# Halved copies at the end of a two-layer kernel, and a new table of due times and engine choices

## The chip, the core and the metric

The kernel runs on one core of a Trainium2 chip. What is measured is device time in microseconds (us), from the start of the program on the core to its end. Five engines work side by side, each through its own list of instructions in order: TensorE (PE: matmuls; PEld: its weight loads), VectorE (DVE), ScalarE (ACT), GpSimd (POOL) and SyncE (SP), which here issues all transfers.

## The reference

Three stages follow one another, all in float32:

```python
state = alpha[:, :, t, :, None] * state + einsum('bhd,bhe->bhde', k[:, :, t], v[:, :, t])
y[:, :, t] = einsum('bhd,bhde->bhe', q[:, :, t], state)          # B=4, H=8, S=768, D=48
x = y as 3072 tokens x 384
h = x @ w_in;  g = (a0 + a1 h + a2 h^2 + a3 h^3) / (1 + |b0||h| + |b1|h^2 + 1e-6);  x = g @ w_out
h = x @ w2_in; g = h * tanh(softplus(h));                                           out = g @ w2_out
```

Both layers have 2048 hidden columns. The weights come as 64-bit floats.

## The kernel before, in words

**The tiles.** The sequence is cut into 6 chunks of 128 positions; with 4 batches a chunk is 512 tokens. A phase (l, c) is layer l on chunk c: 16 steps of 128 hidden columns. In a step `hidden_mms` makes nine matmuls of 512 columns (L653: a high and a low part of x, a high and a low part of the weight) into one of the banks 2 to 4; `hidden` puts the activation on it; `split_g` splits the result into a high part (a cast, L221 on ACT or L223 on DVE) and a low part (a subtraction, L214 on DVE or L216 on POOL); `out_mms` makes nine matmuls (L702) into the sums in banks 5, 6 and 7. Twelve phases run in the order of `PHASES`: (0,0), (0,1), (1,0), (0,2), (1,1), (0,3) and so on to (1,5).

**Attention.** `attn_unit` does one pair of batches of one chunk. Its steps hang on one another: six levels (1, 2, 4, 8, 16, 32) of small matmuls (L462), each followed by DVE work (L477 or L471 scales the operands for the next level, L497 copies the result under a mask) or by ACT copies (L492 at level 16, L486 at level 32); then transposes (L526), their copies (L530), an outer product (L541, copied by L565 in chunk 0), the outputs (L576), their copies (L633), transposes back (L526) and copies into xf (L637), from which L223 and L647 make the high and low parts xh and xl that L653 reads. The units of chunk 0 come first. The first one works in the tile `pair`, the second in banks 2 and 3 (its tiles live inside `zp`, `xg` and `u`). The third unit, of chunk 1, works in `pair` again.

**Weights.** `load_w` brings in one of 32 blocks (L327) and makes float32 of 64-bit words: L328 on ACT, then by the letter in `E_CV` either three DVE steps (D: L330, L332, L334) or two on ACT and one on DVE (A: L341, L342, L344). A cast (L221 or L223 by `E_HC`) gives the high part, a subtraction (L214) or two matmuls and copies (L352, L353, L356) the low part, and both are stored for the later phases.

**The order.** Nobody writes the instructions down in the order in which they stand. Each operation is put into a `Plan` with an engine, a cost and a due time; `Plan.order` then walks through time with those costs, gives each free engine the ready operation that is due first, and the instructions are emitted in the order that comes out. Due times come from a table of numbers (`T_PH`, `AT_P`, `D_X`, `LAG` and others); strings of letters choose engines (`E_M`, `E_GL0`, `E_GL1` by chunk, `E_CV` and `E_HC` by weight block). Between the small matmuls of the start the plan puts fill matmuls (L746). Each engine follows its list strictly: whatever waits holds up all that stands behind it.

**The end.** `evacuate` copies the three banks of sums into `u` (bank 6 on DVE, 5 and 7 on ACT) and issues one store for each.

## Time and profile before

| | us |
|---|---|
| runs of the kernel | 1008.17, 1003.24, 1002.68 (median 1003.24) |
| the profiled execution's own time | 1004.26 |
| its span | 1001.6 |
| PE busy | 969.1 (97%) |
| DVE busy | 668.6 (67%) |
| ACT busy | 622.4 (62%) |
| POOL busy | 263.6 (26%) |

The span runs from the first to the last recorded instruction or transfer; 2.66 us of the profiled execution lie around it. In rows of the trace a number of instructions stands behind an x; a matmul of float32 data counts as two records. A time in brackets is how long the engine stood idle before the row, and the name behind the arrow is what ended that. "issue" means that the profile shows nothing that it waited for. PEclk is the granted clock of TensorE: 1.00 is 2.4 GHz, 0.50 is 1.2 GHz.

### The profile page before, as it was taken

The page shows a single profiled execution, that of the slowest core. Times are in us where ns is not written, and L with a number is a line of the kernel's source. Part 1 is how long each engine was busy: PE and PEld are TensorE (multiplying, and loading weights), DVE is VectorE, ACT ScalarE, POOL GpSimd, SP SyncE. Part 2 cuts the span into 40 slices and gives each one's busy share as a digit, 9 for nine tenths or more (in the row PEclk, how much of TensorE's full clock was granted, in tenths as well). Part 3 has the DMA queues.
Part 4 walks back from the last instruction along what each step waited for, and adds up shares of the span by engine and source line. Part 5 has one row for each costly group of instructions (what it writes and reads, how often), then busy time and mean ns, then how long its engine had stood idle before and what let it go on. Part 6 is the DMA issues. An engine that isn't in the chain of part 4 may idle for free.

```text
span 1001.6 us, 24480 instructions
## 1 busy us (share of the span) xinstructions
PE 969.1 (97%) x10376; PEld 784.4 (78%) x10376; DVE 668.6 (67%) x867; ACT 622.4 (62%) x1051; POOL 263.6 (26%) x202
## 2 busy tenths in 40 slices
PE   7998999899999999999999999999999999999998
PEld 5776877678788878788878888878788878888886
DVE  5668799999997789954589634699952389400211
ACT  2587999699969698622399723396621299633332
POOL 3023675454100044200277700153300000133000
PEclk9799999999999999999999999999999999999999
DMA  7266549756588868557736764848456454565530
GB/s 293 98 222 270 199 151 326 252 164 206 203 292 311 309 230 277 173 191 225 255 97 222 228 210 135 293 153 263 117 167 190 143 156 143 142 214 150 172 111 31
DMA packets 75756, 199.98 MB, mean 200 GB/s; under 512 B 8192, under 2 KB 34944, under 8 KB 74112
## 3 DMA queue, kind: packets, MB, share of 16 engines
q1 hardware_dynamic: 75648, 198.43, 60.3%
q8 instruction: 81, 1.33, 0.5%
q14 instruction: 27, 0.22, 0.1%
HBM read 166.94 MB, written 31.46 MB: 198 GB/s over the span
## 4 chain that ended last, share of the span: by engine, by line
PE 68%; DVE 11%; ACT 9%; issue 3%; DMA 3%; POOL 1%; DVEq 0%; ACTq 0%; POOLq 0%
PE bank L702 31%; PE bank L653 30%; PE pair L462 4%; DVE zp L686 2%; DVE zp L677 1%; DVE zp L679 1%; DVE gg L214 1%; ACT zp L674 1%; DVE qka L477 1%; PE pair L612 1%; ACT u L668 1%; DMA qka<-in_qka_dram 1%; ACT gg L221 1%; ACT zp L681 1%; POOL zp L675 1%
## 5 line engine op out<-in xcount | busy, mean ns | idle before, releaser
L702 PE MATMUL bank<-gg,wo 128*128 128x512 f32 x1728 | 428.5, 392 | 1.9 <-DVE gg L214 0.8
L702 PEld LDWEIGHTS bank<-gg,wo 128*128 128x128 f32 x1728 | 321.0, 188 | 70.4 <-DVE gg L214 1.5
L653 PE MATMUL bank<-xh,wih 128*128 128x512 f32 x576 | 230.8, 401 | 4.9 <-DVE zp L679 2.3
L653 PE MATMUL bank<-xl,wih 128*128 128x512 f32 x576 | 225.6, 392 | 2.3 <-DVE xl L647 2.3
L653 PE MATMUL bank<-xh,wl 128*128 128x512 f32 x576 | 225.9, 392 | 0.5 <-DVE wl L214 0.5
L690 ACT ACTIVATE zp<-bank 128x512 f32<-128x512 f32 x96 | 57.4, 597 | 197.7 <-PE bank L653 196.1
L675 POOL TENSOR_TENSOR zp<-zp,u 128x512 f32<-128x512 f32 x80 | 125.2, 1571 | 160.0 <-ACT zp L674 159.5
L214 DVE TENSOR_TENSOR gg<-zp,gg 128x512 fp32r<-128x512 f32 x144 | 101.6, 710 | 95.3 <-ACT gg L221 90.4
L653 PEld LDWEIGHTS bank<-xh,wih 128*128 128x128 f32 x576 | 108.7, 189 | 30.2 <-DVE zp L679 2.7
L653 PEld LDWEIGHTS bank<-xl,wih 128*128 128x128 f32 x576 | 108.9, 189 | 24.4 <-DVE xl L647 3.1
L653 PEld LDWEIGHTS bank<-xh,wl 128*128 128x128 f32 x576 | 108.6, 189 | 24.1 <-DVE wl L214 1.0
L216 POOL TENSOR_TENSOR gg<-zp,gg 128x512 fp32r<-128x512 f32 x48 | 69.8, 1456 | 217.9 <-ACT gg L221 209.5
L221 ACT CAST gg<-zp 128x512 fp32r<-128x512 f32 x144 | 89.2, 621 | 46.2 <-PE bank L702 31.4
L550 POOL TENSOR_TENSOR tmp<-X,qk 48x768 f32<-48x768 f32 x19 | 30.3, 1595 | 232.3 <-DVE X L555 148.8
L677 DVE SCALAR_TENSOR_TENSOR zp<-zp,sc,bank 128x512 f32<-128x512 f32 x96 | 70.9, 742 | 22.3 <-ACT zp L676 19.8
L686 DVE SCALAR_TENSOR_TENSOR zp<-zp,sc 128x512 f32<-128x512 f32 x80 | 75.5, 949 | 6.4 <-ACT zp L685 5.5
L681 ACT ACTIVATE zp<-zp,c 128x512 f32<-128x512 f32 x96 | 69.4, 725 | 14.3 <-POOL zp L675 14.2
L462 PEld LDWEIGHTS pair<-qka 48*64 48x64 f32 (+4 forms) x3840 | 55.1, 129 | 27.8 <-issue 11.1
L676 ACT ACTIVATE zp<-bank,sc 128x512 f32<-128x512 f32 x96 | 66.1, 688 | 13.4 <-PE bank L653 10.3
L679 DVE SCALAR_TENSOR_TENSOR zp<-zp,sc,bank 128x512 f32<-128x512 f32 x96 | 71.1, 744 | 2.5 <-ACT u L668 0.7
L462 PE MATMUL pair<-qka 48*64 48x32 f32 (+4 forms) x3840 | 62.0, 215 | 6.2 <-DVE AT L497 3.3
L668 ACT ACTIVATE u<-bank 128x512 f32<-128x512 f32 x96 | 56.8, 596 | 15.8 <-PE bank L653 12.1
(124 smaller groups left out, 983.3 us busy)
## 6 DMA issues: line engine op xcount, KB each, us to landing
wo<-woD SPq DMA_DIRECT2D x160, 384.0 KB, 3.3
wl<-wlD SPq DMA_DIRECT2D x160, 192.0 KB, 2.5
qka<-in_qka_dram SPq DMA_DIRECT2D x10, 1536.0 KB, 7.8
woD<-wo SPq DMA_DIRECT2D x16, 768.0 KB, 4.9
raw<-in_w1o_dram SPq DMA_DIRECT2D x8, 768.0 KB, 4.9
raw<-in_w1i_dram SPq DMA_DIRECT2D x8, 768.0 KB, 5.2
wlD<-wl SPq DMA_DIRECT2D x16, 384.0 KB, 4.6
raw<-in_w2i_dram SPq DMA_DIRECT2D x8, 768.0 KB, 5.6
```

Source lines behind the costliest of these rows:

```text
L214: dve(n, due, reads, writes, lambda: nc.vector.tensor_tensor(**kw()))
L216: pool(n, due, reads, writes, lambda: nc.gpsimd.tensor_tensor(**kw()))
L221: act(n, due, reads, writes, lambda: nc.scalar.copy(out=out(), in_=in_()), src="s")
L462: nc.tensor.matmul(bk[j][o:o + m, 32 * g:32 * g + 32].rearrange("p (n l) -> p n l", l=L), lhsT=K[h, e * HC:e * HC + m], rhs=Qv[h, e, :, 1, :],
L653: nc.tensor.matmul(bank[hb], lhsT=w[:, k * P:(k + 1) * P], rhs=x[k], start=(k == 0 and j == 0), stop=(k == KT - 1 and j == 2))
L668: act(NTOK, due, [kh, "tab"], [ku], lambda: nc.scalar.activation(u, h, AF.Abs), table="ln")
L675: pool(NTOK, due, [ku], [kz], lambda: nc.gpsimd.tensor_tensor(out=zs[r], in0=zs[r], in1=u, op=ALU.mult))
L677: dve(NTOK, due, [kh], [kp], lambda: nc.vector.scalar_tensor_tensor(out=ps[r], in0=ps[r], scalar=A2, in1=h, op0=ALU.add, op1=ALU.mult), po ...
L679: dve(NTOK, due, [kh], [kp], lambda: nc.vector.scalar_tensor_tensor(out=ps[r], in0=ps[r], scalar=A1, in1=h, op0=ALU.add, op1=ALU.mult), po ...
L681: act(NTOK, due, [], [kz], lambda: nc.scalar.activation(zs[r], zs[r], AF.Ln, bias=c_1), src="s", ptr=1, table="ln")
L686: dve(NTOK, due, [kw], [kp], lambda: nc.vector.scalar_tensor_tensor(out=ps[r], in0=ps[r], scalar=A0, in1=w(), op0=ALU.add, op1=ALU.mult), ...
L702: nc.tensor.matmul(bank[5 + k], lhsT=wos[b][:, w, k * P:(k + 1) * P], rhs=x[q], start=(f == 0 and j == 0), stop=(f == FT - 1 and j == 2))
```

## The change

The last phase's sums are copied in halves of 256 columns, the left half by ACT, the right half by DVE, and each half has a store of its own: six instead of three. The table of numbers is another one, the plan counts a table load of ACT at the first conversion of layer 0, and eight strings and numbers choose other engines. Cut to the core:

```diff
-T_PH = (8.402, 4.683, 4.572, 7.535, 7.065, 5.706, 9.463, 9.341, 5.182, 6.904, 4.724, 3.344)
+T_PH = (8.402, 4.739, 4.796, 7.6, 7.065, 5.962, 9.494, 9.394, 5.212, 7.04, 4.831, 2.283)
...
-E_M = 'PPPPPV'
-E_GL0 = 'PVVPVV'
-E_GL1 = 'VVVVPV'
+E_M = 'PPVPPV'
+E_GL0 = 'PVVVVV'
+E_GL1 = 'VPVPPV'
...
-E_CV = 'ADAAAAAAAAAAAADADDDDDADDDAAAAAAAA'
+E_CV = 'ADAAAAAAADAAADADDDDDADDDAADDDADA'
...
+LOADED0 = None
...
-        out, busy, loaded = [], {}, "ln"
+        out, busy, loaded = [], {}, LOADED0
...
-        act(n, due, [kr], [ks], lambda: nc.scalar.activation(st, mag, AF.Copy, scale=F64_SHIFT), src="s")
+        act(n, due, [kr], [ks], lambda: nc.scalar.activation(st, mag, AF.Copy, scale=F64_SHIFT), src="s",
+            table="ln" if l == 0 else None)
...
+            if (l, c) == PHASES[-1]:
+                plan.readers[f"u{j}b"] = plan.readers.get(f"u{j}", []) + [plan.writer[f"u{j}"]]
+                for n, t in enumerate((slice(0, NTOK // 2), slice(NTOK // 2, NTOK))):
+                    ku = f"u{j}" + "b" * n
+                    if n:
+                        dve(NTOK // 2, due, [f"bank{5 + k}"], [ku], lambda k=k, j=j, t=t: nc.vector.tensor_copy(
+                            out=us[j][:, t], in_=bank[5 + k][:, t]), port=False)
+                    else:
+                        act(NTOK // 2, due, [f"bank{5 + k}"], [ku], lambda k=k, j=j, t=t: nc.scalar.copy(
+                            out=us[j][:, t], in_=bank[5 + k][:, t]))
+                    dma(131, due, [ku], [], lambda k=k, j=j, t=t: nc.sync.dma_start(out=out[c][:, k, t], in_=us[j][:, t]))
+                continue
```

Further numbers of the table (`AT_P`, `LAG`, `D_SPL`, `W_LEAD`, `X_LEAD`, `D_W2`, `D_X`, `D_EV`) and letters of `E_HC` change in the same manner. What the table does is seen in the lists of the engines. Line numbers of the change are 1 to 14 higher than those of before: L334 becomes L336, L477 L479, L497 L499, L341 L343, L486 L488, L633 L635.

**Place 1: DVE in the first 25 us.** `qka0` and `pair` belong to the first unit, `zp` and `bank2`, `bank3` to the second, `f321` is the buffer of the first weight block. Before:

```order
L477 TENSOR_TENSOR qka0_145<-qka0_145 128x2x256x2
L471 TENSOR_TENSOR zp_134<-zp_134 128x1024
L497 COPY_PREDICATED zp_134<-cst_65,bank2_127 128x256
L497 COPY_PREDICATED AT0_144<-cst_65,pair_126 128x128x4
L497 COPY_PREDICATED zp_134<-cst_65,bank3_128 128x256
L477 TENSOR_TENSOR qka0_145<-qka0_145,qk0_148 128x2x128x4
L334 SCALAR_TENSOR_TENSOR f321_102<-raw1_100,f321_102 128x768
```

In the change:

```order
L479 TENSOR_TENSOR qka0_145<-qka0_145 128x2x256x2
L336 SCALAR_TENSOR_TENSOR f321_102<-raw1_100,f321_102 128x768
L473 TENSOR_TENSOR zp_134<-zp_134 128x1024
L479 TENSOR_TENSOR qka0_145<-qka0_145,qk0_148 128x2x128x4
L499 COPY_PREDICATED AT0_144<-cst_65,pair_126 128x128x4
L499 COPY_PREDICATED zp_134<-cst_65,bank2_127 128x256
```

The last step of the block's conversion moves from behind the first unit's level 4 (the row with 128x2x128x4) to ahead of it, and the second unit's copies under the mask move behind it.

**Place 2: ACT at the second unit's level 32.** The four rows that end in 32x8x32 copy that level's result out of banks 2 and 3. Before:

```order
L633 COPY vn0_146<-pair_126 128x384
L492 COPY zp_134<-bank3_128 16x8x16
L356 CAST wl2_89<-bank7_132 128x384
L341 ACTIVATE zb0_103<-raw0_99 128x768
L356 CAST wl2_89<-bank5_130 128x384
L637 COPY xf_105<-pair_126 128x3x128 x2
L328 ACTIVATE f320_101<-raw0_99 128x768
L486 COPY zp_134<-bank2_127 32x8x32
L342 ACTIVATE zb0_103<-raw0_99,c_f_69 128x768
L486 COPY zp_134<-bank3_128 32x8x32
```

In the change:

```order
L635 COPY vn0_146<-pair_126 128x384 x2
L343 ACTIVATE zb0_103<-raw0_99 128x768
L488 COPY zp_134<-bank2_127 32x8x32
L358 CAST wl2_89<-bank7_132 128x384
L488 COPY zp_134<-bank3_128 32x8x32
L639 COPY xf_105<-pair_126 128x3x128 x2
L488 COPY zp_134<-bank2_127 32x8x32
L358 CAST wl2_89<-bank5_130 128x384
L488 COPY zp_134<-bank3_128 32x8x32
L329 ACTIVATE f320_101<-raw0_99 128x768
```

The copies move ahead of conversion steps (L328 and L342 of before) that they stood behind.

**Place 3: the last copies.** `bank_130`, `bank_131` and `bank_132` are banks 5, 6 and 7. The waits in brackets name the engines or transfers whose semaphores the instruction waits for. ACT in the change:

```order
L722 COPY u<-bank_130 128x256 [waits DMAHW4_49,PE_49]
L722 COPY u<-bank_131 128x256 [waits DMAHW5_49,PE_49]
L722 COPY u<-bank_132 128x256 [waits DMAHW6_49,PE_49]
```

DVE in the change:

```order
L719 COPY u<-bank_130 128x256 [waits DMAHW4_49,Activation_49]
L719 COPY u<-bank_131 128x256 [waits DMAHW5_49,Activation_49]
L719 COPY u<-bank_132 128x256 [waits DMAHW6_49,Activation_49]
```

Before, ACT copied two whole banks and DVE one, and each of these copies waited for PE. In the change ACT's halves wait for PE and DVE's halves wait for ACT.

## Rows read from the trace of the kernel before

**Rows 1.** Windows by stage: length; busy PE, PEld, DVE, ACT, POOL; PEclk; DMA share, GB/s.

```profile
84.50:175.80 91.30, 86.27 (x1324) 67.81 (x1323) 80.04 (x95) 84.61 (x142) 54.75 (x40) 0.98 0.64 227
175.80:251.20 75.40, 70.89 (x836) 56.70 (x837) 70.49 (x86) 62.76 (x118) 35.18 (x26) 0.98 0.62 204
251.20:339.50 88.30, 87.34 (x920) 71.07 (x919) 74.95 (x97) 72.39 (x117) 5.35 (x7) 1.00 0.79 283
339.50:409.80 70.30, 69.67 (x781) 55.76 (x779) 63.55 (x86) 60.16 (x103) 27.69 (x17) 1.00 0.77 252
...
490.00:558.40 68.40, 67.34 (x772) 54.18 (x772) 57.67 (x64) 59.44 (x103) 42.66 (x29) 1.00 0.59 185
```

**Rows 2.** Timeline of DVE, 18 to 29 us: start, length, engine, line.

```profile
18.71 1.27 DVE L477 TENSOR_TENSOR qka<-qka 128x1024 f32<-128x1024 f32 x1
...
25.62 0.70 DVE L497 COPY_PREDICATED AT<-cst,pair 128x512 f32<-128x512 int32 x1 [3.77 <-PE pair L462]
...
27.91 0.94 DVE L334 SCALAR_TENSOR_TENSOR f<-raw,f 128x768 int32<-128x768 int32 x1
```

**Rows 3.** Timeline of ACT at 28.9 us.

```profile
28.89 0.83 ACT L221 CAST wo<-f 128x768 fp32r<-128x768 f32 x1 [5.28 <-DVE f L334]
```

**Rows 4.** Timeline of PE, 22 to 39 us.

```profile
22.62 1.24 PE L746 MATMUL bank<-cst 128*128 128x256 f32 x5 [2.96 <-issue]
23.79 1.78 PE L462 MATMUL pair<-qka 48*60 48x32 f32 x64
25.50 3.78 PE L746 MATMUL bank<-cst 128*128 128x256 f32 x8
29.21 1.93 PE L462 MATMUL bank<-zp 48*64 48x32 f32 x64
30.94 1.70 PE L462 MATMUL pair<-qka 48*56 48x32 f32 x64
32.57 5.30 PE L746 MATMUL bank<-cst 128*128 128x256 f32 x12
37.80 0.92 PE L462 MATMUL pair<-qka 48*48 48x32 f32 x64
```

**Rows 5.** Window of the slow clock.

```profile
24.00:36.00 12.00, 12.00 (x208) 10.05 (x204) 7.76 (x10) 1.40 (x2) 0.00 (x0) 0.50 0.35 132
```

**Rows 6.** ACT by line and form, whole span: busy, mean ns of one, idle before.

```profile
L328 ACT ACTIVATE f<-raw 128x768 f32<-128x768 f32 x32 | 29.2, 913 | 18.2 <-DMA raw<-in_w1i_dram 9.8 <-DMA raw<-in_w1o_dram 6.2 <-DMA raw<-in_w2o_dram 2.1
L342 ACT ACTIVATE zb<-raw,c_f 128x768 uint16<-128x768 uint16 x22 | 25.7, 1169 | 0.1
L341 ACT ACTIVATE zb<-raw 128x768 f16<-128x768 f32 x22 | 23.7, 1079 | 0.1
...
L356 ACT CAST wl<-bank 128x384 fp32r<-128x384 f32 x6 | 2.9, 479 | 0.2
```

**Rows 7.** Timeline of ACT: the first unit's and the second unit's last copies.

```profile
48.38 1.07 ACT L530 COPY qka<-pair 128x512 f32<-128x512 f32 x2
...
66.06 0.98 ACT L486 COPY zp<-bank 32x256 f32<-32x256 f32 x3
```

**Rows 8.** Timeline of PE at the first hidden matmul.

```profile
84.52 1.03 PE L462 MATMUL pair<-qka 48*56 48x32 f32 x64
85.48 0.50 PE L653 MATMUL bank<-xh,wih 128*128 128x512 f32 x1
```

**Rows 9.** DVE by line and form, whole span.

```profile
L214 DVE TENSOR_TENSOR gg<-zp,gg 128x512 fp32r<-128x512 f32 x144 | 101.6, 710 | 95.3 <-ACT gg L221 90.4 <-PE bank L702 3.4
...
L671 DVE SCALAR_TENSOR_TENSOR zp<-zp,sc,u 128x512 f32<-128x512 f32 x16 | 11.9, 748 | 1.7 <-ACT zp L670 1.6
```

**Rows 10.** Timeline of the end, and the last stores' time to landing.

```profile
997.30 0.69 DVE L713 COPY u<-bank 128x512 f32<-128x512 f32 x1 [4.05 <-PE bank L702]
997.98 0.58 ACT L715 COPY u<-bank 128x512 f32<-128x512 f32 x1 [0.77 <-PE bank L702]
...
out_dram<-u SPq DMA_DIRECT2D x3, 256.0 KB, 2.1
```

More of the change, by code (lines that the diff above doesn't have):

```diff
@@ L39 @@
 PHASES = ((0, 0), (0, 1), (1, 0), (0, 2), (1, 1), (0, 3), (1, 2), (0, 4), (1, 3), (0, 5), (1, 4), (1, 5))
-T_PH = (8.402, 4.683, 4.572, 7.535, 7.065, 5.706, 9.463, 9.341, 5.182, 6.904, 4.724, 3.344)
+T_PH = (8.402, 4.739, 4.796, 7.6, 7.065, 5.962, 9.494, 9.394, 5.212, 7.04, 4.831, 2.283)
 AT_P0 = (0.318, -13.418, 0.649)
 AT_P1 = (0.292, 1.189, 0.288)
-AT_P = (0.573, 0.916, 0.31)
+AT_P = (0.576, 0.985, 0.276)
 D_MID = 10.219
-LAG = (32.081, 10.172)
-D_SPL = (-7.368, 6.936)
-W_LEAD = 4.738
-X_LEAD = 96.57
+LAG = (31.971, 10.172)
+D_SPL = (-1.971, 5.762)
+W_LEAD = -3.689
+X_LEAD = 69.333
 D_W1 = (0.495, 18.655)
-D_W2 = (17.835, 18.763)
+D_W2 = (20.572, 23.284)
 E_LO = 'VV'
 E_TREE, E_QK = ('PPPVPV', 'VVVVVP')
-E_M = 'PPPPPV'
-E_GL0 = 'PVVPVV'
-E_GL1 = 'VVVVPV'
+E_M = 'PPVPPV'
+E_GL0 = 'PVVVVV'
+E_GL1 = 'VPVPPV'
 R_PSUM = 'R.....'
@@ L61 @@
 E_LW = 'PVPPPVVVVVVVVVVVVVVVVVVVVVVVVVVV'
-E_HC = 'AAVVVVVVAAVAAAAVVVAVAVAAVVVAVAAA'
+E_HC = 'AAVVVVVVAAVAAAAAAAAVVAAAAVVVVAVV'
 E_X0 = 'V'
-E_CV = 'ADAAAAAAAAAAADADDDDDADDDAAAAAAAA'
+E_CV = 'ADAAAAAAADAAADADDDDDADDDAADDDADA'
 R0 = (39.706, 10.751)
 NRAW, NF32 = 2, 2
-D_X = 86.568
-D_EV = -19.693
+D_X = 75.469
+D_EV = -9.067
 PAD_FROM = 290.0
```

## The prediction

> **What bounds the kernel now.** I read the windows by stage first, because the share of PE over the whole span hides where it loses. In the stage of the first layer's first chunk PE is busy 86.27 us of 91.30, in the next 70.89 of 75.40; after that it loses 0.96, 0.63 and, in a later one, 1.06 us a stage [rows 1]. From 251 us on PE has next to nothing to give, so an order that changes there can hardly gain, only lose. What can be gained lies ahead of the first hidden matmul at 85.48 us, where small matmuls, DVE and ACT wait for each other in turn.
>
> So I read the timelines of that start, DVE first. DVE ends level 2 of the first attention unit about 19.9 us, then stands 3.77 us until PE has done level 4, and the last step of the first weight block, L334, stands behind that and begins only at 27.91 [rows 2]. ACT, with the cast of that block next in its list, has waited 5.28 us by then [rows 3]. PE loses 2.96 us ahead of 22.62 for a reason that the profile calls issue, then works through five records of fill matmuls before level 4 at 23.79; level 8 begins at 30.94 and level 16 at 37.80, each behind fill matmuls and the second with 5.30 us of them ahead of it [rows 4]. After the lost 2.96 us the granted clock is 0.50, that is 1.2 GHz, from 24 to 36 us, though PE is busy throughout [rows 5]. All of this is a chain: what comes earlier in it brings the first hidden matmul earlier.
>
> **The start, step by step.** The reader should count every step against the same event of before.
>
> *L334* moves ahead of level 4 (place 1). Only rows that DVE does anyway before 20 us stand ahead of it, so it begins at about 19.9 instead of 27.91, 8.0 us earlier, and so does the cast behind it on ACT. SP's next load into that buffer waits for L334 too and moves with it. This is not yet 8.0 us for the kernel: the attention units wait for PE.
>
> *PE.* I assume that the 2.96 us stay, since the transfers ahead of them are issued in the same order, and that the slow clock stays after them. In the change level 4 stands right behind the second unit's level 1, so it begins at about 22.65. The next distances are from starts [rows 4]: level 4 takes 1.71 (25.50 - 23.79), a fill matmul of two records 0.88 (5.30 / 6), the second unit's level 2 takes 1.73 (30.94 - 29.21), level 8 takes 1.63 (32.57 - 30.94). The change has five fill matmuls, then level 8, then three fill matmuls and the second unit's level 2, then level 16. So level 8 begins at 22.65 + 1.71 + 4.40 = 28.8 (before 30.94), level 16 at 28.8 + 1.63 + 2.64 + 1.73 = 34.8 (before 37.80). At the slow clock it takes about 1.6 and ends at 36.4, against 38.72: **2.3 us earlier**. DVE's steps between them fit under the fill matmuls.
>
> *ACT to the first unit's copies.* From the end of level 16 to the end of L530 ACT is busy without a break before; it ends at 48.38 + 1.07 = 49.45 [rows 7]. The change puts one L341, one L342 and one L356 more and one L328 less into this stretch: 1.08 + 1.17 + 0.48 - 0.91 = 1.8, or 1.6 with the tenth by which neighbours overlap [rows 6]. It gives 2.3 - 1.6 = **0.7 us earlier**.
>
> *ACT to the second unit's level 32.* From there to the last L486 before takes 67.04 - 49.45 = 17.6 us [rows 7]. Counted in the two orders, the change does one L328, one L341, two L342 and one L356 less in this stretch, those being done before or put behind the copies (place 2). That is 0.91 + 1.08 + 2.34 + 0.48 = 4.8 us [rows 6], 4.3 without the overlaps. With ACT the engine that never rests here, it is **4.3 us earlier**, so 5.0 in all. What is late next is the second unit's last round: transposes, outer product, outputs, transposes back. ACT's conversions that were put behind now lie in its pauses; I take this part as 0, between 1 us of gain and 1 us of loss.
>
> *Given back.* Before, the third unit's level 8 is done ahead of the first hidden matmul (1.03 us, [rows 8]); in the change that matmul group is only level 4, and level 8 comes later. PE must do it all the same: **1.0 us back**. The first hidden matmul comes at about 80.5 instead of 85.48, and of that 4.0 us stay.
>
> **The engine choices.** In phase (0,2), from 340 us, the multiplication goes from POOL to DVE: the order has L671 15 times more in that stage, 15 x 0.748 = 11.2 us, less an estimated 5.8 of attention steps that move to the stages beside it, on 63.55 of 70.30 busy us of DVE [rows 1, 9]. In the stage from 490 us DVE gets 11 subtractions, 11 x 0.710 = 7.8, on 57.67 of 68.40. In the one from 251 us four blocks are converted by DVE instead of ACT, at least 4 x 0.94 [rows 2], on 74.95 of 88.30. DVE stays below each stage's length; as PE has losses of 0.63 to 1.06 us there, I take 0, with up to 2 us of gain if the losses of the two stages ahead of 251 us shrink, and a rival below for the loss. Elsewhere POOL takes subtractions from DVE in stages where both have room: nothing, covered by steps of PE that are longer than either.
>
> **The last copies.** Before, ACT copies bank 7 in 0.58 us after the last matmul [rows 10]. Halves at once would save some 0.2 us. But DVE's half waits for ACT, and for nothing of PE (place 3); it can only know that the bank is complete through ACT's half of the same bank. So the halves come one after the other: ACT between 0.29 (half of 0.58) and 0.48 (384 columns, [rows 6]), DVE between 0.35 (half of 0.69) and 0.69; about 0.37 + 0.43 plus 0.05 for the semaphore makes 0.85, **0.25 us later** than the 0.58. The last store is half as large; its 2.1 us to landing [rows 10] may shrink by some tenths. The sum of the end is 0.1 us later, between 0.3 earlier and 0.5 later; six stores instead of three are issued while the matmuls of the other banks still run.
>
> The Trainium skill, PSUM — Partial Sum Buffer, section "PSUM bank collisions raise a hardware error", says that two engines must not touch one bank in the same quadrant of partitions at once, not even to read disjoint columns. By it the wait is needed, and the halves at once would not be open to any order of this kernel; had they run at once, the end would come 0.45 us earlier than in my sum. No run here shows a collision.
>
> **The sum.** -0.7 - 4.3 + 1.0 + 0.1 = -3.9 us. The profiled execution took 1004.26, so it gives 1000.4; the median of the runs lies 1.02 below that execution, and so my forecast is 999.3 us.
>
> **The rivals.** *The start gains nothing.* The slow clock lasts longer, or a load or PE's lost 2.96 us grows by what DVE saves. For it: 12 us of slow clock with PE fully busy [rows 5] show that the clock does not follow the work at once, and each of the 10 fill matmuls in this stretch costs 0.88. Against it: ACT's shorter list does not hang on PE's clock. Between 0 and 1 us is left: 1002 to 1004.
>
> *More than my sum.* If PE does not lose the 2.96 us, the clock stays and the start gains the whole 8.0 of L334, less 1.0: 1003.24 - 7.0 = 996.2. Against it: nothing in the change lightens the transfers of the start.
>
> *DVE becomes the bound, the case on the other side.* The stage from 176 us shows what it costs when DVE is busy 70.49 of 75.40, 93%: PE loses 4.51 us [rows 1]. In the change the stages from 251, 340 and 490 us come close to that load or pass it (for the second (63.55 + 11.2 - 5.8) / 70.30 = 98%). If each then loses 4.51 instead of 0.96, 0.63 and 1.06, that is 3 x 4.51 - 2.65 = 10.9 us, and the result is 999.3 + 10.9 = 1010.2. If one of them does so, the gain is gone (1003), if two, 1006. It decides once DVE's busy share passes some 93% while attention levels still wait for it. Against it: from 340 us DVE was 90% busy and PE lost 0.63.
>
> *The change does not do what it says.* For the halves at once I hold this to be so, and it is in the sum.
>
> **How the numbers follow.** My forecast gets 0.47, with 996.5 to 1002 as its own range; a start without gain 0.18; more than the sum 0.14; DVE the bound in one or two stages 0.12, in all three 0.09. No change that is measurable here means within 0.5%, 5.0 us: 998.2 to 1008.3. Faster than that are the 0.14 and some 0.18 out of the forecast's 0.47, and a little from the others: 0.33. Slower is the last case, 0.09. The rest is 0.58. The range holds forecast, the start without gain, most of the larger gain and one or two stages bound by DVE: 993.5 to 1006.0. It leaves out the last case and some 0.08 at the lower end.
>
> **What would show it.** Right: L334 near 20 us and ACT's cast right behind it; level 16 at about 35; the last L486 of the second unit at about 62; the first hidden matmul near 80.5; the stages after 251 us with PE losses near a microsecond; at the end DVE's half beginning after ACT's half of the same bank. Wrong, if the first hidden matmul stays near 85, if the clock stays at 0.50 beyond 40 us, if a stage after 251 us loses over 3 us of PE, or if both halves of a bank begin together.

## The result and the profile after

| | before | after |
|---|---|---|
| median of the runs, us | 1002.96 (4 runs, 999.71 to 1008.17) | 991.15 (4 runs, 989.64 to 993.89) |
| ratio to before | | 0.9876, 95% interval 0.9845 to 0.9906 |
| the profiled execution, us | 1004.26 | 993.89 |
| its span, us | 1001.6 | 992.1 |
| first hidden matmul, us | 85.48 | 79.07 |

The change makes the kernel 1.24% faster, 11.8 us, three times what was forecast, and the time lies below the range. The profiled executions differ by 10.4 us: 9.5 in the span, and 0.9 around it (2.66 us before, 1.79 after; as it varies from 1.7 to 3.1 between executions of the kernel before, this account leaves it out). The other 1.4 of the 11.8 us is spread: the profiled execution lies 1.3 us above the median before, and 2.7 above it after. In the code of the change all lines from L329 on stand one to fourteen further than before (L334 is now L336, L462 is L464, L647 is L649, L653 is L655, L702 is L704).

The windows by stage, as in [rows 1], cut at the first hidden matmul and then where DVE begins each split of x (the low part, L647 before, L649 in the change):

```profile
0.00:79.07 79.07, 68.10 (x1638) 54.85 (x1638) 55.17 (x69) 46.76 (x76) 18.12 (x25) 0.96 0.66 239
79.07:171.48 92.41, 86.23 (x1326) 68.35 (x1324) 85.15 (x94) 83.11 (x140) 56.12 (x40) 0.98 0.62 219
171.48:242.20 70.72, 67.14 (x823) 52.85 (x824) 63.89 (x83) 61.71 (x117) 32.16 (x27) 1.00 0.68 220
242.20:330.66 88.46, 88.32 (x924) 71.77 (x923) 85.39 (x112) 66.28 (x111) 9.04 (x7) 1.00 0.78 276
330.66:400.16 69.50, 69.11 (x782) 56.21 (x781) 67.00 (x91) 57.99 (x102) 2.79 (x2) 1.00 0.78 248
...
915.79:992.10 76.31, 72.06 (x318) 59.34 (x317) 15.10 (x23) 24.06 (x41) 1.30 (x1) 1.00 0.36 105
```

The same cuts before fall at 85.48, 175.84, 251.16 and 925.87 us. By these borders the 9.5 us are 6.4 at the start; 2.55 in the two stages behind it, of which the first gave back 2.0 (92.41 after 90.36) and the second gained 4.6 (70.72 after 75.32); 1.1 from there to 925.87; and 0.6 lost at the end (76.31 after 75.73).

These borders do not stand at the same work. Up to 242.20 us the change has begun 511 of its 3456 matmuls of 512 columns (L655 and L704 together, one record each; called the large matmuls below), up to 251.16 the kernel before 523: 12 matmuls of 0.39 us, 4.7 us, were left for later, as much as the second stage gained, and some 60 small ones (level 8 of the third unit) were taken in. A cut at equal work is the place where 748 of them have been begun, 311.07 us before and 304.05 after. From there to the beginning of the last one:

```profile
311.07:997.55 686.48, 680.05 (x5956) 554.44 (x5955) 406.45 (x551) 376.90 (x633) 152.23 (x105) 1.00 0.60 188
304.05:987.46 683.41, 679.96 (x5956) 554.42 (x5955) 400.75 (x555) 369.37 (x625) 141.22 (x105) 1.00 0.61 188
```

The first row is before, the second after. So the 9.5 us are 6.4 at the start, 0.6 from the first hidden matmul to this cut, 3.1 behind it and 0.6 lost at the end. Behind the cut PE has the same number of matmuls, the same busy time and the same clock in both; what went is idle time, 3.45 us after 6.43. Before, six waits of PE for DVE, of 0.35 to 0.90 us, make up 3.84 us there, these two among them:

```profile
410.56 0.50 PE L653 MATMUL bank<-xl,wih 128*128 128x512 f32 x1 [0.75 <-DVE xl L647]
525.06 0.30 PE L526 MATMUL pair<-cst,qka 128*128 128x128 f32 x1 [0.90 <-DVE qka L477]
```

After, four waits for DVE are left, of 0.19 to 0.30 us, and one of 1.51 us, which both kernels have.

In the two stages up to 242.20 us (251.16 before) PE is not idle for less, 9.76 us after 9.54, but it loses less to slow clock. Before, the second of them has these two windows of ten microseconds, the clock being the third number from the right:

```profile
170.00:180.00 10.00, 7.14 (x26) 5.11 (x27) 9.86 (x13) 7.83 (x19) 4.06 (x3) 0.88 0.69 271
180.00:190.00 10.00, 10.00 (x161) 8.03 (x160) 8.71 (x11) 5.20 (x15) 6.69 (x8) 0.95 0.71 213
```

They lose 1.2 + 0.5 = 1.7 us of PE's work. PE's timeline before shows what stood ahead of them:

```profile
174.50 0.49 PE L653 MATMUL bank<-xh,wih 128*128 128x512 f32 x1 [0.54 <-ACT xh L221]
176.58 0.50 PE L653 MATMUL bank<-xl,wih 128*128 128x512 f32 x1 [1.58 <-DVE xl L647]
...
177.38 0.52 PE L653 MATMUL bank<-xl,wih 128*128 128x512 f32 x1
177.70 0.63 PE L653 MATMUL bank<-xh,wl 128*128 128x512 f32 x1
```

PE waits for ACT's and DVE's part of the split, and behind that a matmul takes 0.63 instead of 0.39 us. After the change PE comes to the same place so:

```profile
170.38 0.49 PE L704 MATMUL bank<-gg,wo 128*128 128x512 f32 x1 [0.44 <-POOL gg L217]
171.62 0.50 PE L704 MATMUL bank<-gg,wo 128*128 128x512 f32 x1 [0.75 <-DVE wo L215]
171.96 0.40 PE L655 MATMUL bank<-xh,wih 128*128 128x512 f32 x1
172.22 0.50 PE L655 MATMUL bank<-xl,wih 128*128 128x512 f32 x1
```

No wait at the split, and the clock stays at 2.4 GHz for the whole stage (PEclk 1.00 from 171.48 to 242.20 us). At the start, PE's timeline (compare [rows 4]) reads:

```profile
22.57 0.25 PE L464 MATMUL bank<-zp 48*64 48x32 f32 x3 [0.86 <-issue]
...
28.22 0.41 PE L464 MATMUL pair<-qka 48*56 48x32 f32 x15 [1.32 <-issue]
28.55 2.03 PE L760 MATMUL bank<-cst 128*128 128x256 f32 x6
30.52 1.94 PE L464 MATMUL bank<-zp 48*64 48x32 f32 x64
32.25 1.48 PE L464 MATMUL pair<-qka 48*48 48x32 f32 x64
```

The pause of 2.96 us is gone; there are shorter ones at other places, in sum no less (4.3 us ahead of the first hidden matmul, before 3.7), and level 16 begins at 32.25 instead of 37.80. The granted clock of the whole start is 0.96 instead of 0.92.

### The profile page after: what moved, and what is told of

The parts are those of the page before. It is cut to its first block, busy times and chain, and to the rows that moved or that the text cites. A ratio compares the mean times of both kernels' runs of the same rounds, so it can differ in the third digit from the quotient of the medians.

```text
span 992.1 us, 24521 instructions
## 1 busy us (share of the span) xinstructions
PE 963.7 (97%) x10370; PEld 780.6 (79%) x10370; DVE 665.5 (67%) x878; ACT 611.0 (62%) x1043; POOL 255.0 (26%) x202
## 4 chain that ended last, share of the span: by engine, by line
PE 72%; DVE 7%; ACT 3%; DMA 2%; issue 1%; DVEq 0%; SPq 0%; ACTq 0%
PE bank L704 34%; PE bank L655 32%; PE pair L464 3%; PE pair L614 2%; DVE zp L688 1%; DMA qka<-in_qka_dram 1%; DVE zp L679 1%; DVE zp L681 1%; PE pair L528 1%; PE pair L543 1%; DMA x2d<-u 1%; DVE AT L499 1%; ACT u L670 1%; DVE gg L215 1%; DVE qka L479 0%
## 5 line engine op out<-in xcount | busy, mean ns | idle before, releaser
L704 PE MATMUL bank<-gg,wo 128*128 128x512 f32 x1728 | 430.2, 393 | 1.5 <-DVE wo L215 0.8
L704 PEld LDWEIGHTS bank<-gg,wo 128*128 128x128 f32 x1728 | 322.1, 188 | 70.4 <-DVE wo L215 1.1
L655 PE MATMUL bank<-xh,wih 128*128 128x512 f32 x576 | 230.2, 400 | 3.3 <-DVE zp L681 1.7
L655 PE MATMUL bank<-xl,wih 128*128 128x512 f32 x576 | 224.9, 390 | 0.2 <-DVE xl L649 0.2
L655 PE MATMUL bank<-xh,wl 128*128 128x512 f32 x576 | 224.6, 390 | 0.0
L217 POOL TENSOR_TENSOR gg<-zp,gg 128x512 fp32r<-128x512 f32 x64 | 90.5, 1415 | 267.3 <-ACT gg L222 123.4
L215 DVE TENSOR_TENSOR gg<-zp,gg 128x512 fp32r<-128x512 f32 x128 | 92.2, 726 | 87.3 <-ACT gg L222 86.7
L677 POOL TENSOR_TENSOR zp<-zp,u 128x512 f32<-128x512 f32 x64 | 98.9, 1549 | 144.6 <-ACT zp L676 144.5
L655 PEld LDWEIGHTS bank<-xh,wih 128*128 128x128 f32 x576 | 108.2, 188 | 29.0 <-DVE zp L681 4.1
L655 PEld LDWEIGHTS bank<-xh,wl 128*128 128x128 f32 x576 | 108.1, 188 | 22.9
L655 PEld LDWEIGHTS bank<-xl,wih 128*128 128x128 f32 x576 | 108.3, 188 | 22.3 <-DVE xl L649 1.4
L464 PEld LDWEIGHTS pair<-qka 48*64 48x64 f32 (+4 forms) x3840 | 54.4, 126 | 30.5 <-issue 12.8
L224 DVE CAST gg<-zp 128x512 fp32r<-128x512 f32 x48 | 22.2, 468 | 74.4 <-ACT zp L692 69.5
L464 PE MATMUL pair<-qka 48*64 48x32 f32 (+4 forms) x3840 | 61.3, 213 | 9.4 <-issue 3.4
```

The costliest lines, as they stand in the source:

```text
L215: dve(n, due, reads, writes, lambda: nc.vector.tensor_tensor(**kw()))
L217: pool(n, due, reads, writes, lambda: nc.gpsimd.tensor_tensor(**kw()))
L464: nc.tensor.matmul(bk[j][o:o + m, 32 * g:32 * g + 32].rearrange("p (n l) -> p n l", l=L), lhsT=K[h, e * HC:e * HC + m], rhs=Qv[h, e, :, 1, :],
L655: nc.tensor.matmul(bank[hb], lhsT=w[:, k * P:(k + 1) * P], rhs=x[k], start=(k == 0 and j == 0), stop=(k == KT - 1 and j == 2))
L677: pool(NTOK, due, [ku], [kz], lambda: nc.gpsimd.tensor_tensor(out=zs[r], in0=zs[r], in1=u, op=ALU.mult))
L704: nc.tensor.matmul(bank[5 + k], lhsT=wos[b][:, w, k * P:(k + 1) * P], rhs=x[q], start=(f == 0 and j == 0), stop=(f == FT - 1 and j == 2))
```

## The experiments

Each time is a median, each ratio one to the runs of before on the same chip (medians 1003.20 us for e_start, e_rest, e_letters and e_whole, 1005.00 for e_nudge, e_delay, e_nofill and e_conv, 1003.41 for the others). Positions in the span are from one profiled execution of each kernel. With the same order the first hidden matmul still lies between 77.2 and 79.3 us from execution to execution (four kernels here share it: the change, e_whole, e_delay, e_letters); with the old start it lies between 85.5 and 86.8 (before, e_oldhead, e_rest). So the 6.4 us of the profiled pair are at the lower end of what the start gains.

### Only the start: e_start

The kernel before with the start's reordering alone:

```diff
-        out, busy, loaded = [], {}, "ln"
+        out, busy, loaded = [], {}, None
...
-        act(n, due, [kr], [ks], lambda: nc.scalar.activation(st, mag, AF.Copy, scale=F64_SHIFT), src="s")
+        act(n, due, [kr], [ks], lambda: nc.scalar.activation(st, mag, AF.Copy, scale=F64_SHIFT), src="s",
+            table="ln" if l == 0 else None)
```

> The kernel before, with nothing of the change but the plan's idea of the loaded table; only the order moves, from the first instructions on. Theory A (the start's gain is the start's own, and about 2 of its 6.4 us are given back before the second chunk): first hidden matmul near 79.1 us, the split of the second chunk near 171.5 instead of 175.8, the next split near 246.8, still 4.4 earlier, and a time near 998.5. Rival B (what the start gains is lost again in the wait ahead of the second chunk, where matmuls wait for DVE's split at 176.6): first hidden near 79, but the next split near 251 and a time of 1002 to 1003. Rival C (the whole gain of the change up to 242 us comes out of the start): next split near 242.2, time near 993.

Measured: 1008.54 us, ratio 1.0059 (1.0033 to 1.0084), **slower** than before. No theory had that. The first hidden matmul comes at 77.39, 8.1 us earlier, and all of it is lost in the two stages behind:

```profile
77.39:175.95 98.56, 89.91 (x1330) 70.88 (x1323) 85.82 (x97) 82.81 (x141) 55.93 (x40) 0.93 0.58 205
175.95:253.57 77.62, 72.87 (x835) 57.52 (x836) 71.20 (x85) 63.70 (x120) 33.77 (x27) 0.96 0.60 197
```

PE is idle for 13.4 us, and the clock of 0.93 and 0.96 costs some 10 more (0.07 x 98.56 + 0.04 x 77.62). This execution took 1012.86 us, the longest of the nine, with a mean granted clock of 0.984; the median of the nine is 0.991, as before. So the share of the clock is overstated here: a median run is 5 us longer than before at the same mean clock.

### All but the start: e_rest

```diff
-LOADED0 = None
+LOADED0 = "ln"
...
-            table="ln" if l == 0 else None)
+            table=None)
```

> The changed kernel with the old start: the plan again takes the table for loaded, all else of the change stays. Theory A: first hidden matmul near 85.5 us with the 2.96 us of lost PE time and a granted clock of 0.50 in 24 to 36 us again, the stage of the second chunk about 70.7 us long as in the change, and a time near 995.6 (the change's 991.2 and 4.4). Rival B: 992 to 993, the start being worth little at the end. Rival C: second chunk's stage 75 us long again, time near 1001.

Measured: 1007.6 us, ratio 1.0046 (1.0024 to 1.0067), also slower than before, and outside all three theories; the first hidden matmul is at 86.81, theory A's place, and the second chunk's stage takes 74.19 us, near rival C's 75. So start and rest, each alone, cost 4 to 6 us; together they gain 11.8. But both runs have a flaw that their expectations overlooked: the planner orders anew everything behind the place where I changed it, so neither is "the old order with one part of the change".

### A shuffle that changes nothing else: e_nudge and b_nudge

In the changed kernel, and then in the one before, one latency of the planner:

```diff
-           "DVE": {"PE": 0.2, "POOL": 0.155, "": 0.128}, "POOL": {"": 0.13}, "SP": {"": 0.15}}
+           "DVE": {"PE": 0.2, "POOL": 0.155, "": 0.138}, "POOL": {"": 0.13}, "SP": {"": 0.15}}
```

> The changed kernel with one latency of the planner for DVE's results 0.010 us longer: no engine choice and no due time is touched, the order up to the first hidden matmul stays, and from there to the end of the first layer's first stages it is shuffled. Theory A (the gain up to 331 us belongs to this one order: any shuffle of it brings back waits of PE of about 2 us each, behind which the granted clock falls to 1.2 GHz): PE idle in the three stages from 79 to 331 us 14 us or more instead of 9.9, some windows of 10 us with a clock of 0.83, time 995 to 1003. Rival B (the gain lies in the choices and due times, not in the single order): idle near 10, one slow window as in the change, time 990 to 993.

> The kernel before with the planner's latency for DVE's results 0.010 us longer, as in the shuffled version of the change. Theory A (the kernel before is one good order too, and its neighbours lose as the change's do): first hidden within 3 us of 85.5, more idle than 10.5 us of PE in the next three stages or more slow windows, time 1006 to 1020. Rival B (only the change is such a point; the old order is an ordinary one): time 999 to 1006.

Measured: e_nudge 1008.98 us, ratio 1.0039 (1.0017 to 1.0060), 16 to 18 us above the change (by the ratios and by the medians); b_nudge 1013.16 us, ratio 1.0103 (1.0078 to 1.0128), 10 us above before. Theory A in both, though e_nudge lost 6 us more than its range allowed (995 to 1003). In e_nudge the start is the change's (first hidden matmul 77.24), then:

```profile
77.24:180.75 103.51, 92.68 (x1334) 73.50 (x1332) 89.01 (x100) 86.50 (x144) 55.58 (x41) 0.92 0.58 206
180.75:254.31 73.56, 68.44 (x820) 54.87 (x821) 64.45 (x81) 62.18 (x117) 33.86 (x29) 0.95 0.64 212
```

One of its waits, on PE's timeline, is an attention level that comes up in PE's list before ACT has copied its operand:

```profile
157.69 1.08 PE L464 MATMUL pair<-qka 48*32 48x32 f32 x64 [4.67 <-ACT AT L494]
```

Of each kernel, before and after, one neighbour was measured, and it lost 10 and 16 to 18 us. To take a part out of such an order one must keep the rest of it fixed.

### Start and rest exchanged with nothing planned anew: e_newhead and e_oldhead

The plan is made twice, once with each start; the list up to the first hidden matmul comes from the one and the rest from the other:

```diff
+        first = min(n for n, o in enumerate(base) if o[0] == "PE" and o[1] == 0.680)
+        (head, hops), (rest, rops) = [self.sort(base, t) for t in (None, "ln")]
+        head = head[:head.index(first)]
+        done = set(head)
+        return ([(hops[n][4], hops[n][7]) for n in head]
+                + [(rops[n][4], rops[n][7]) for n in rest if n < len(base) and n not in done])
```

This is e_newhead, in the kernel before; e_oldhead is the changed kernel with ("ln", None) in that place.

> The kernel before, with the change's order up to the first hidden matmul spliced in front, and behind it the old order word for word (what the new start has done already is left out of it). Nothing is planned anew behind the start. Theory A (the start's gain is worth something by itself, and what made the earlier run with a new start slow was only the new shuffle behind it): first hidden at 77.4 to 79, the next splits 4 to 6 us earlier than 175.8 and 251.2, time 997 to 1000. Rival B (the old order behind it was made for DVE and ACT as the old start leaves them, so the gain is waited away): first split within 2 us of 175.8, time 1002 to 1004. Rival C (work that the old start had done early is now late and stops PE, and the clock falls behind each stop): over 1006.

> The changed kernel with the order of before up to the first hidden matmul spliced in front, and behind it the changed order word for word. Theory A (start and rest add up when nothing is shuffled): first hidden at 85.5 to 87, the stages behind it 90 to 92, 70 to 71 and 88.5 us long as in the change, time 995.5 to 998. Rival B (the changed order fits only its own start): PE idle of more than 14 us in these three stages instead of 9.9, slow windows, time over 1001.

Measured: e_newhead 1000.98 us, ratio 0.9987 (0.9973 to 1.0002); e_oldhead 999.29 us, ratio 0.9957 (0.9935 to 0.9979). For e_newhead that lies between theories A and B; for e_oldhead it is theory A, at 1.3 us above its range. Windows of e_oldhead:

```profile
0.00:86.76 86.76, 73.47 (x1712) 58.28 (x1713) 58.05 (x70) 47.28 (x76) 17.01 (x25) 0.94 0.65 237
86.76:179.27 92.51, 85.17 (x1262) 67.61 (x1260) 84.16 (x95) 83.63 (x141) 56.08 (x40) 0.98 0.57 200
179.27:248.54 69.27, 66.64 (x823) 52.95 (x824) 63.86 (x83) 61.75 (x117) 32.12 (x27) 1.00 0.68 224
```

With the old start the changed rest keeps its stages, 92.51 and 69.27 us, with a clock of 1.00 in the second. So the new rest takes 161.78 us for these two stages with the old start and 163.13 with the new one, where the old rest took 165.68; part of that difference is the work left for later at its end. The new start is worth its whole size only with the new rest: 8.1 us by the ratios (0.9957 to 0.9876), with the old one 1.3. With the old rest, PE's timeline of e_newhead (its lines are 9 further than before) shows why:

```profile
77.72 0.40 PE L471 MATMUL pair<-qka 48*60 48x32 f32 x10 [0.77 <-issue]
80.12 1.72 PE L471 MATMUL pair<-qka 48*56 48x32 f32 x64 [1.99 <-DVE AT L506]
81.77 0.79 PE L662 MATMUL bank<-xh,wih 128*128 128x512 f32 x1
82.36 0.63 PE L662 MATMUL bank<-xl,wih 128*128 128x512 f32 x1
```

The old rest still has level 8 of the third unit ahead of the first hidden matmul, as in [rows 8]. With the new start DVE has not got so far; PE waits 1.99 us for it, and the next matmuls run at 1.2 GHz. The first hidden matmul comes at 81.77, not at 77 to 79; the first stage loses 2.4 us more (92.72 after 90.36) and the second 1.2 (76.54 after 75.32), so that the next split, at 251.03, stands where it stood before. This execution was the longest of the twelve (1003.38), so the median keeps some gain.

### A wait put in: e_delay

```diff
-            dve(NTOK, due, keys + [f"xh{k}"], [f"xl{k}"], lambda k=k: nc.vector.tensor_tensor(
-                out=xl[k], in0=src[:, k, :], in1=xh[k].bitcast(F32), op=ALU.subtract))
+            times = 4 if k == 0 and due == V[FT] - D_X else 1
+            dve(NTOK, due, keys + [f"xh{k}"], [f"xl{k}"], lambda k=k, times=times: [nc.vector.tensor_tensor(
+                out=xl[k], in0=src[:, k, :], in1=xh[k].bitcast(F32), op=ALU.subtract) for _ in range(times)])
```

> The changed kernel with the first subtraction of the second chunk's split written four times, so that PE's first matmul of that stage waits 3 x 0.63 = 1.9 us longer near 172 us; all else stays in its order. Theory A (a wait of PE there costs itself and then the clock, as before the change): matmuls of 0.63 instead of 0.39 us behind the wait, a window of 170 to 180 or 180 to 190 us at 0.83 to 0.88, the next split at about 242.2 + 1.9 + 1.7 = 245.8, time near 994.8. Rival B (only the wait): clock stays 1.00, next split 244.1, time near 993. Rival C (absorbed by waits that follow): next split 242.2 to 243, time near 991.2.

Measured: 995.06 us, ratio 0.9902 (0.9873 to 0.9930); theory A, forecast 994.8. The intervals of this ratio and the change's overlap, so it is the trace that decides. Theory A's place for the next split, 245.8, did not come: it stands at 244.21, rival B's number, but only since the split before it began 2.2 us earlier in this execution (169.30 after 171.48); the stage in between is 4.2 us longer, as in theory A. PE's timeline of that place (lines 1 further than in the change):

```profile
169.44 0.50 PE L705 MATMUL bank<-gg,wo 128*128 128x512 f32 x1 [0.73 <-DVE wo L215]
...
172.22 0.50 PE L656 MATMUL bank<-xl,wih 128*128 128x512 f32 x1 [2.05 <-DVE xl L650]
...
172.79 0.58 PE L656 MATMUL bank<-xh,wih 128*128 128x512 f32 x1
173.17 0.63 PE L656 MATMUL bank<-xl,wih 128*128 128x512 f32 x1
...
176.16 0.44 PE L656 MATMUL bank<-xh,wl 128*128 128x512 f32 x1
```

and its windows:

```profile
169.30:244.21 74.91, 69.77 (x823) 55.15 (x824) 65.08 (x86) 61.90 (x117) 32.73 (x27) 0.95 0.63 207
170.00:180.00 10.00, 7.95 (x87) 6.14 (x87) 8.66 (x12) 5.08 (x17) 4.75 (x4) 0.83 0.53 187
190.00:200.00 10.00, 10.00 (x157) 7.69 (x157) 6.74 (x9) 8.06 (x15) 5.42 (x4) 0.83 0.59 202
```

A wait of 2.05 us brings the picture of before back: matmuls of 0.63 us, 1.7 us lost in the window, and a second slow stretch behind two later waits of 0.92 and 1.05 us. The stage takes 74.91 instead of 70.72, nearly the 75.32 of before. So at this place a wait cost itself and as much again, in one execution. The Trainium skill, TensorE: Matmul & The Clock Gate, section "HAM oscillation — how this bites in real kernels", describes the slow clock as a price that its example kernel pays anew behind each of its waits for DMA. The rows of this run agree for the wait of 2.05 us; behind one of 1.96 us at 92.44 us the clock stays at 1.00.

### One step of the prediction by itself: e_l334

In the kernel before, the third DVE step of the second weight block is put where the change has it, ahead of the second unit's level-1 product:

```diff
+        out.remove(self.late)
+        out.insert(out.index(self.mark), self.late)
         return [(ops[n][4], ops[n][7]) for n in out]
```

> The kernel before with one instruction moved: the third DVE step of the second weight block (L334 of before) stands ahead of the second unit's level-1 product, at about 19.9 us instead of 27.9, as in the change; nothing else moves. Theory A (the prediction's first step: this instruction holds back the cast on ACT and SP's load, and by them the start): the cast at about 21 instead of 28.9, first hidden matmul 2 to 5 us earlier than 85.5, time 998 to 1001. Rival B (the start is set by PE's order and its clock, and this step is covered): cast at 21, but first hidden within 1 us of 85.5 and clock 0.50 in 24 to 36 us, time 1002 to 1005. Rival C (the load that it sets free takes transfers from others): first hidden later than 86.5.

Measured: 1002.13 us, ratio 1.0003 (0.9979 to 1.0026); rival B by the time and the first hidden matmul, but not by the clock, which it had at 0.50 from 24 to 36 us (measured 0.89). ACT's timeline (lines up to 6 further than before):

```profile
23.34 0.81 ACT L223 CAST wo<-f 128x768 fp32r<-128x768 f32 x1
...
62.05 0.98 ACT L492 COPY zp<-bank 32x256 f32<-32x256 f32 x3
...
83.16 0.86 ACT L643 COPY xf<-bank 128x384 f32<-128x384 f32 x2 [1.89 <-PE bank L532]
```

The cast is 5.5 us earlier than in [rows 3], and the second unit's last level-32 copies are 4.0 us earlier than in [rows 7], but the copies into xf come at 83.16 after 82.57 before, and the first hidden matmul at 86.07. PE lost the gain on the way:

```profile
70.24 0.44 PE L466 MATMUL pair<-qka 48*64 48x32 f32 x17 [1.86 <-issue]
70.61 4.54 PE L752 MATMUL bank<-cst 128*128 128x256 f32 x12
...
82.41 0.24 PE L466 MATMUL pair<-qka 48*60 48x32 f32 x1 [1.93 <-issue]
```

That the earlier copies are the work of this one instruction is not shown, as the clock is also 1.00 from 28 to 70 us in this execution, and e_oldhead, which has the old start untouched, reaches the same copies at 62.23.

### The fill matmuls left out: e_nofill

```diff
     def warm():
-        nc.tensor.matmul(bank[4][:, 0:2 * P], lhsT=ident, rhs=cst[:, 0:2 * P], start=True, stop=True)
+        pass
```

> The changed kernel without the fill matmuls of the first 60 us, whose results nothing reads; the rest of the order stays. Theory A (they hold the clock up, and the start needs it): granted clock near 0.50 in most of 20 to 60 us, levels of 1.7 to 1.9 us instead of 1.1, first hidden matmul at 82 or later, time 994 or more. Rival B (they stand in PE's way: the pauses of PE called issue and the slow clock behind them come from the records that they add): no pause over 1 us, levels 8 and 16 of the first unit 1 to 3 us earlier, first hidden at 75 to 77.5, time near 989. Rival C (ACT's list sets the pace of the start, PE's clock is hidden under it): first hidden within 1 us of 79.1 though the clock is low.

Measured: 999.7 us, ratio 0.9939 (0.9915 to 0.9962), first hidden matmul at 84.61: theory A by the time, but not by the place. Windows of the start:

```profile
16.00:40.00 24.00, 18.73 (x521) 15.50 (x518) 21.59 (x27) 13.66 (x19) 2.84 (x6) 1.00 0.49 181
...
50.00:60.00 10.00, 9.67 (x174) 7.80 (x175) 5.12 (x7) 5.76 (x16) 0.00 (x0) 0.53 0.89 318
60.00:70.00 10.00, 4.71 (x136) 3.89 (x134) 5.49 (x6) 9.89 (x14) 1.86 (x2) 0.64 0.53 193
70.00:84.61 14.61, 11.19 (x295) 10.22 (x295) 11.57 (x15) 5.56 (x9) 4.30 (x7) 0.50 0.91 335
```

Up to 40 us the clock stands at 1.00 without them, where before it fell to 0.50 with them [rows 5]; from 50 us on it is 0.50 to 0.64 without them. By level 16 this start is still ahead (29.70 us, in the change 32.25), so they earn their place in the second half of the start. Its twelve runs spread from 994.17 to 1001.43 us, eight of them above 998; the profile is of one of these eight.

### Choices of engine: e_conv and e_letters

e_conv sets the two strings for the weight blocks back, e_letters the three for the multiplication and the subtractions:

```diff
-E_HC = 'AAVVVVVVAAVAAAAAAAAVVAAAAVVVVAVV'
+E_HC = 'AAVVVVVVAAVAAAAVVVAVAVAAVVVAVAAA'
-E_CV = 'ADAAAAAAADAAADADDDDDADDDAADDDADA'
+E_CV = 'ADAAAAAAAAAAADADDDDDADDDAAAAAAAA'
```

```diff
-E_M = 'PPVPPV'
-E_GL0 = 'PVVVVV'
-E_GL1 = 'VPVPPV'
+E_M = 'PPPPPV'
+E_GL0 = 'PVVPVV'
+E_GL1 = 'VVVVPV'
```

> The changed kernel with the old choices for converting weight blocks: block 9 and three late ones by ACT and DVE together again, and the copies of blocks 15 to 17 to the matmul's type by DVE again. The start stays. Theory A (DVE is what PE waits for at 93, 185 and in the old order at 176 us, so 3 x 0.55 us of copies back on DVE and conversions in another place bring waits back): splits of the second chunk at 172 to 174 and of the next at 245 to 248, time 994 to 998. Rival B (any order but the tuned one loses, whatever the choice): as much lost as by a shuffle alone. Rival C (nothing depends on them): split at 242 to 243, time 991 to 992.

> The changed kernel with the old engine choices for the multiplication and for the two layers' subtractions; the first 350 us are in the changed order. Theory A (the choices are worth only what the stages after 242 us gained, 1.1 us): first hidden at 79.1, split at 242.2 as in the change, last split near 917, time 991 to 992.5. Rival B (the choices carry the gain of these stages and more): PE idle of 0.6 to 1 us a stage again from 242 us on, time 994 to 995. Rival C (DVE's higher load costs something in the change): time under 990.5.

Measured: e_conv 1004.82 us, ratio 1.0014 (0.9990 to 1.0038). That is as much as a shuffle costs (rival B), so nothing follows on the choice itself. e_letters keeps the change's order for 330 us (its split there begins at 330.71 after 330.66) and so tells something: 995.36 us, ratio 0.9923 (0.9893 to 0.9952); its profiled execution takes 1.5 us more than the change's behind that split. That is nearly one wait, of 1.58 us for DVE's split at 403.71 us, which the change does not have; from the cut at equal work to the last matmul it takes 685.04 us after 683.41. Between theory A and rival B nothing is decided: the trace is near A's 1.1 us, the medians differ by 4 us, as in B, with intervals that overlap.

### The sums copied whole: e_whole

```diff
-            if (l, c) == PHASES[-1]:
+            if False:
```

> The changed kernel with the last phase's sums copied whole again, by one engine each, and stored in three transfers; the rest of the order is that of the change. Theory A (serial halves cost the end): from the end of the last matmul to the span's end 3.6 us as before instead of 4.2, last stage 75.7 instead of 76.3, time about 0.6 us under the change, which is within the spread of its runs. Rival B (the halves gain): 4.5 us or more after the last matmul, time 0.3 us or more above the change.

Measured: 991.88 us, ratio 0.9897 (0.9864 to 0.9929), not to be told from the change. The trace shows theory A: 3.60 us from the last matmul to the end (its last row of L704 ends at 984.70, the span at 988.3), in the change 4.25 (987.85 to 992.1). DVE's timeline of the change:

```profile
987.62 0.43 DVE L719 COPY u<-bank 128x256 f32<-128x256 f32 x1 [0.25 <-ACT u L722]
988.29 0.42 DVE L719 COPY u<-bank 128x256 f32<-128x256 f32 x1 [0.25 <-ACT u L722]
```

and the stores' row of the listing of the line:

```profile
L724 SPq DMA_DIRECT2D out_dram<-u x6: 338/396/406, 986.9 to 989.3; - x6
```

Each of DVE's halves waits for ACT's, so the last bank takes 0.86 us from the last matmul (987.85 to 988.71) instead of 0.6. SP then issues the last store only at 989.3, 0.6 us later, being busy with the one before (its last four issues begin at 987.83, 988.33, 988.83 and 989.3, from 0.25 to 0.6 us behind the end of their copies); in e_whole it issues it at 985.4, right behind the copy's end at 985.33.

### All kernels side by side

The two stages behind the first hidden matmul, from the windows of each profile (idle is length less busy PE; the loss to the clock is length x (1 - PEclk), to some 0.5 us):

| kernel | first hidden | two stages | PE idle | lost to the clock | time |
|---|---|---|---|---|---|
| before | 85.48 | 165.68 | 9.5 | 3.3 | 1002.96 |
| after | 79.07 | 163.13 | 9.8 | 1.8 | 991.15 |
| e_whole, same order there | 77.16 | 162.12 | 9.2 | 1.8 | 991.88 |
| e_oldhead | 86.76 | 161.78 | 10.0 | 1.9 | 999.29 |
| e_newhead | 81.77 | 169.26 | 9.2 | 7.7 | 1000.98 |
| e_rest | 86.81 | 167.65 | 12.7 | 3.7 | 1007.6 |
| e_start | 77.39 | 176.18 | 13.4 | 10.0 | 1008.54 |
| e_conv | 78.78 | 171.53 | 15.0 | 7.6 | 1004.82 |
| e_nudge | 77.24 | 177.07 | 16.0 | 12.0 | 1008.98 |
| b_nudge | 83.83 | 172.43 | 13.8 | 8.8 | 1013.16 |

The column of the two stages is to be read with care: at its end the kernels have begun from 511 (after, e_whole, e_oldhead, e_conv) to 523 (before, e_newhead) of the large matmuls, at 0.39 us each. The stretch behind the cut at equal work (748 of the large matmuls begun) up to the last one holds the same matmuls in all kernels of the next table, at a clock of 1.00:

| kernel | rest | stretch | PE idle |
|---|---|---|---|
| before | old | 311.07 to 997.55: 686.48 | 6.4 |
| e_newhead | old | 311.03 to 997.56: 686.53 | 6.2 |
| e_l334 | old | 311.25 to 997.63: 686.38 | 6.3 |
| after | new | 304.05 to 987.46: 683.41 | 3.4 |
| e_whole | new | 301.14 to 984.32: 683.18 | 3.2 |
| e_oldhead | new | 310.43 to 993.68: 683.25 | 3.4 |
| e_delay | new | 306.04 to 989.08: 683.04 | 3.2 |
| e_nofill | new | 309.79 to 992.96: 683.17 | 3.3 |
| e_letters | new, old letters | 304.06 to 989.10: 685.04 | 4.9 |

So the 3.1 us behind the cut belong to the new rest, whatever the start, and the clock has no part in them.

## Why the prediction was wrong, step by step

**L334 and the cast**: right in place (21.25 and 22.24 us; forecast 19.9 and right behind it), but worth nothing measurable by itself (e_l334, within 0.3%).

**PE at the start**: the assumption that the 2.96 us and the slow clock stay failed; the pause broke up, and the slow clock moved to 30 to 40 us (0.68 there). Level 16 came at 32.25, not 34.8, and the end of L530 (now L532) at 45.73, so the term of 0.7 was 3.7 us. Where these pauses and the slow clock fall changes from execution to execution, so part of it is chance.

**ACT's shorter list**: forecast 4.3, measured 4.6 (from 45.73 to the end of the last level-32 copy at 58.71, 13.0 us; before 17.6). The counting of instructions between two events held.

**The second unit's last round**, taken as 0, lost 1.9: from there to the first hidden matmul 20.4 us, before 18.4.

**Given back**: 1.0 forecast, 2.0 measured. With that the next split stood 4.4 us earlier where 4.0 were forecast; up to 171 us errors of both signs cancelled, by luck.

**The step that failed** is the zero for everything between there and the end ("I take 0, with up to 2 us of gain if the losses of the two stages ahead of 251 us shrink"), and the sentence that it rests on, that an order that changes from 251 us on "can hardly gain, only lose". Cut at equal work, the stretch up to 311 us gained 0.6 us where the given-back 1.0 was forecast as a loss, and the stretch behind it 3.1 where 0 was. Nearly all of these 3.1 us are PE's waits for DVE, each of 0.35 to 0.90 us before. I had read them in [rows 1] as losses of 0.63 to 1.06 us a stage, taken them as too small to give anything and not added them up: PE is idle for 6.43 us in this stretch before. Ahead of 311 us it was the clock behind the waits that shrank (by 1.7 us, in this pair of executions), which [rows 1] only hints at with 0.98. And I priced start and rest apart: the rest alone gives 4.3 us by the ratios, with either start the same in the trace, but the start alone 1 to 2, and both 11.8.

**The end**: copies one after the other as forecast (0.86 us for 0.85), but 0.6 us lost instead of 0.1, since the last store had to wait for SP, a queue that I had not priced. I had taken the six stores as issued while matmuls still run; three of them are issued behind the last matmul's end at 987.85. The Trainium skill, PSUM — Partial Sum Buffer, section "PSUM bank collisions raise a hardware error", asks that one half wait for the other. The trace shows no two halves of a bank at once.

**The rivals**: DVE as the bound did not occur. In the stage from 242.20 us DVE is busy 85.39 of 88.46, 97%, and PE idle for 0.14 us. The point of 93% that I read from the stage at 176 us was no threshold; at 96% and 97% (67.00 of 69.50 us from 330.66) PE hardly waited, so DVE's load alone does not decide it. "More than my sum", 996.2 with a chance of 0.14, named the right direction and part of the reason, the PE pause that breaks up. **The range** ended at 993.5 because nothing behind the start was allowed to gain more than 2 us; by this account it gained 3.7, and the start 1.4 more than forecast.

What stays open: which of the due times and choices took the waits behind 311 us away (the three strings of e_letters account for 1.6 of the 3.1 us in one execution); what PE waits for in the pauses called issue; and why one wait is followed by a slow stretch and another of equal length is not (a wait of 1.95 us at 93 us, with the same order, goes with a clock of 0.83 from 90 to 100 us in the change and of 1.00 for the whole stage in e_delay).

## What to carry to other kernels

Where a planner orders the work, a profile of one execution shows where PE waits and where the clock is low behind it, and a change of the order should be read first at those places: was the operation that PE waited for moved ahead? A part of such a change can only be measured with the rest of the order held fixed; to plan anew with a part undone measures a shuffle, which here cost 10 to 18 us. Compare stages at borders of equal work of the engine that bounds them: at a border that itself moves in the order, work left for later looks like a gain. Add up the small waits of all stages before calling them nothing. And price a wait ahead of a dense stretch of matmuls at its length plus the slow stretch that the rows show behind it.

## What the runs showed of the hardware

- A wait of 2.05 us of PE, with 0.45 and 0.73 us of waits shortly before it, was followed by matmuls of 0.63 instead of 0.39 us from 172.8 to 176.2 us (e_delay, clock 0.83 from 170 to 180 us); in the same execution one of 1.96 us at 92.44 us was not (clock 1.00 from 90 to 100 us).
- With DVE busy for 97% of a stage, PE was idle for 0.14 us in all (the stage from 242 us).
- PE's pauses called issue add up to 4.3 us ahead of the first hidden matmul in the change, and to 6.0 in e_l334 (0.90, 1.31, 1.86 and 1.93), and move between executions of the same order (at 28.22 us 1.32 in the change, at 27.44 us 0.50 in e_whole).
- Without fill matmuls the clock stood at 1.00 from 16 to 40 us, and at 0.50 from 70 to 84.61 us (e_nofill, one execution).
- SP issues the small stores at the end 0.44 to 0.50 us apart, each of 0.34 to 0.41 us; the last of six halves is issued 0.6 us after its copy, where the last of three whole ones is issued right behind it.
